# Seven-product matrix scheme in a gated MLP: the output's last block moved from second to last

## The chip, the cores and the metric

The kernel runs on one core of a Trainium2 chip. The metric is the device time of one execution in microseconds (us).

## What is computed

Eight batches of 448 tokens go through a sigmoid attention and then through a gated MLP. Cut to what matters:

```python
scores = q @ k.T / sqrt(64) - log(448)           # 12 heads, head_dim 64
x = sigmoid(scores) @ v                          # 448 x 768 per batch
h = relu(x @ w_in)                               # 448 x 1024
u, v = h[:, :512], h[:, 512:]
v_s = w_spatial @ normalised(v) + b_spatial      # over the tokens
out = (u * v_s) @ w_out                          # 448 x 768
```

Everything is float32. On TensorE a float32 product is made from three products of rounded parts: high x high, low x high and high x low.

## The kernel before

Batches are taken in pairs, m = 0 to 3. A pair goes through attention (scores psc, values pav), through the gate's products (pv, pg), then through the products for u (PSUM tiles ux, uy) and last through the output's products (PSUM tiles o). Pair 0 uses plain products; pairs 1 to 3 use a scheme that makes a 2 x 2 block product from seven block products. Only these three pairs are touched here.

**The scheme.** Both factors are cut into 2 x 2 blocks. For the output, the rows are the 512 channels of the gated values in halves, the columns are the two batches b0 and b1. The weight blocks are called 11, 12, s2, s3, s1, s4 and 22 (s1 to s4 are sums of blocks, made once and kept in DRAM). Each meets one block of the other factor: 11 meets G11, 12 meets G21, s2 meets T2, s3 meets T3, s1 meets T1, s4 meets G22, and 22 meets T4. The gated blocks are G11, G21, G12 and G22, where the first digit is the channel half and the second the batch; T1 = G12 - G11, T3 = G22 - G12, T2 = T3 + G11 = G22 - T1, T4 = G21 - T2. Products 11, s2, s1 and s4 add up in one PSUM sum X, products 12, s3 and 22 add up in another, Y, and after some of them the running sum is copied out, to be added to the other sum later. `by_blocks` (L836) runs through the seven; for the output each has three row blocks i = 0, 1, 2 of six matmuls, so 18 matmuls. X and Y of one i are the two halves of one PSUM tile `o_i`.

**Where the gated blocks come from.** `gated_by_blocks` (L859) does the same with u's weights (two row blocks i, nine matmuls each). Its results, gated by VectorE (`gate`, L898), are ready in the order G11, G22, G12 and last G21. Its local `then` issues the VectorE and ScalarE work after each product: copies and additions of the running sums (r1, r2, r3), the gate, `high` (ScalarE rounds a block to its high part, L901) and `low` (VectorE subtracts the high part, L905). What is not urgent is a generator `rest` (L907) put into a list of jobs, and `spare(n)` takes n steps from it.

**The output.** `output_by_blocks` (L967) has its own `then`: after product 11 it copies the running sum X to r1, after 12 it adds Y to r1 and sends the row to DRAM, and so on; `between` runs after the last row block of s3 and issues the next pair's loads (`more_loads`: a value load, one attention load, another value load) and `next_splits` (six VectorE instructions that split the next pair's first three attention inputs). At L1020 on, each row is sent to DRAM as it is ready.

**What sets the order.** Every engine runs its instructions in the order in which the code issues them (`in_program_order`), and waits on semaphores. SyncE (SP) issues all loads and stores, in order. Seven weight blocks share four places in SBUF: block n + 4 is loaded once block n's product is through (`load_block`). The work tiles come from pools with a few buffers under a tag: raw (4), v (2), tmp (3); a new tile takes the buffer that was given up first and waits for its last reader. The gated blocks sit in the program's tiles `g_2_0` (G11), `g_2_2` (G21), `g_3_0` (G12) and `wval_s` (G22) for pair 1; `ur_1_0`, `ur_1_1`, `ur_1_2` are the running sums.

Of the kernel before, what the change touches and what calls it, by code (L numbers as in the profile page):

```python
# [8 lines left out]
F32 = mybir.dt.float32  # L9
# [26 lines left out]
def attn_gmlp_kernel(  # L36
# [412 lines left out]
    ORDER = ("11", "12", "s2", "s3", "s1", "s4", "22")  # L449
# [24 lines left out]
    def keep_plain(w7, w):  # L474
        for name in NAMES:
            if name in ORDER:
                at = NAMES.index(name) * BLOCK
                nc.sync.dma_start(w7[ORDER.index(name)], w[:, :, at : at + BLOCK].bitcast(F32))

    def output_weight_sums(stage):  # L480
# [13 lines left out]
        def finish(i, name):  # L494
            nc.vector.tensor_sub(low(i).bitcast(F32R), low(i), high(i).bitcast(F32))
            nc.sync.dma_start(w7_out[ORDER.index(name)], stage[:, i])

# [33 lines left out]
    def weight_sums():  # L531
# [14 lines left out]
        keep_plain(w7_u, w_u[0])  # L546
# [288 lines left out]
    PRODUCTS = (("11", X), ("21", W), ("t2", X), ("t3", Y), ("t1", X), ("22", X), ("t4", Y))  # L835

    def by_blocks(flat, stationary, moving, nk, ps, then):

        started = set()
        for pos, (mv, to) in enumerate(PRODUCTS):  # L840
            w = block(flat, pos)
            ops = [(a, k, c) for k in range(nk) for a, c in TERMS]
            for i, out_ps in enumerate(ps[to]):
# [10 lines left out]
                then(pos, i)  # L854
# [5 lines left out]
    def gated_by_blocks(m):  # L860
# [106 lines left out]
    def output_by_blocks(m, final, between):  # L967
# [5 lines left out]
        spare_u = sums.pop("r")[2]  # L973
# [4 lines left out]
        r1 = [spare_u[:, 0], spare_u[:, 1], in_wval(2)]  # L978
        later = {}

        def pieces(name, last):
            t = work.tile([P, 2, 512], F32, tag="tmp", name=f"o{name}_{m}", bufs=3)
            later[name] = [t[:, 0, :S], t[:, 1, :S], in_wval(last)]
# [10 lines left out]
        def then(pos, i):  # L994
            mv = PRODUCTS[pos][0]
            if mv == "11":
                spare(1)
                nc.scalar.copy(r1[i], px[i])  # L998
            elif mv == "21":
                if not i:  # L1000
                    spare(1)
                nc.vector.tensor_add(r1[i], py[i], r1[i])
                leave(b0, i, 0, r1[i])
                spare(1)
                if i == n - 1:
                    spare(99)
                    pieces("r3", 0)
                    pieces("c12", 1)
                    pieces("r2", 2)
            elif mv == "t2":  # L1010
                nc.scalar.copy(later["r2"][i], px[i])
            elif mv == "t3":
                if i == n - 1:
                    between()
            elif mv == "t1":
                r3 = later["r3"][i]
                nc.scalar.copy(r3, px[i])
                nc.vector.tensor_add(r3, py[i], r3)
                leave(b1, i, 1, r3)
            elif mv == "22":  # L1020
                nc.scalar.copy(later["c12"][i], px[i])
                leave(b1, i, 0, later["c12"][i])
            elif mv == "t4":
                r2 = later["r2"][i]
                nc.vector.tensor_add(r2, py[i], r2)
                leave(b0, i, 1, r2)
# [268 lines left out]
    for m in range(B // 2):  # L1295
        if m == 1:
            stage = const.tile([P, 4, 2, BLOCK], F32, tag="w_u", name="stage")
            keep_plain(w7_out, w_out_s)
# [36 lines left out]
        if m:  # L1335
# [86 lines left out]
```

## Time and profile before

| what | value |
|---|---|
| median of three runs | 660.47 us (659.56 to 660.82) |
| the profiled execution | 661.15 us |
| its span | 659.3 us |
| TensorE busy, share of the span | 642.7 us, 97% |
| VectorE busy | 450.5 us, 68% |
| ScalarE busy | 324.9 us, 49% |
| chain that ended last | PE 91%, DVE 6%, ACT 2%, DMA 1% |

The profile names engines PE (TensorE), PEld (its weight loads), DVE (VectorE), ACT (ScalarE), POOL (GpSimd) and SP (SyncE, with its queue SPq). Ends of matmuls are modelled, so a matmul's duration in a row is longer than the step from one to the next. The chain that ended last is followed back from the last instruction to what released it; its share by engine says who set the time. TensorE is nearly always busy, so what is to be looked for is where it is not, and where it is busy at less than full clock.

### The profile page before, as it was taken

What the parts mean: (1) busy time and instruction counts of PE and PEld (TensorE: products, weight loads), DVE (VectorE), ACT (ScalarE), POOL (GpSimd) and SP (SyncE); (2) the same over time, 40 slices, a digit from 0 to 9 for tenths busy, and PEclk for the clock granted to TensorE, in tenths of its full rate; (3) what the DMA queues carried; (4) which work ended last, traced back from release to release, by engine and by line L of the source; (5) the groups of instructions that cost most, each with busy time, mean ns of one, the idle gap of its engine ahead of it and who ended that gap; (6) DMA issues with size and microseconds to landing.
All of it is one profiled execution on the core that took longest, in us unless ns stands there. A gap on an engine that the chain in (4) does not pass through costs nothing.

```text
span 659.3 us, 10184 instructions
## 1 busy us (share of the span) xinstructions
PE 642.7 (97%) x4154; PEld 495.3 (75%) x4154; DVE 450.5 (68%) x629; ACT 324.9 (49%) x410; POOL 28.8 (4%) x63
## 2 busy tenths in 40 slices
PE   8999999999999999997999999999799999999977
PEld 3645889999754588996966658899696666889966
DVE  4989789849478887839476638674836754777562
ACT  5986322323777845224268745512427774542231
POOL 0000010000000002000000002200000000210000
PEclk9999999999999999998999999999799999999989
DMA  8764113565862491044744460012574465002144
GB/s 294 242 200 173 55 41 95 153 247 197 302 241 75 163 366 54 1 144 147 278 171 171 164 277 0 1 49 95 178 275 143 171 229 211 1 1 92 52 141 171
DMA packets 29952, 99.90 MB, mean 152 GB/s; under 512 B 3152, under 2 KB 9808, under 8 KB 29904
## 3 DMA queue, kind: packets, MB, share of 16 engines
q1 hardware_dynamic: 29472, 98.89, 41.6%
q8 instruction: 33, 0.54, 0.3%
q10 hardware_dynamic: 432, 0.34, 0.2%
q14 instruction: 15, 0.12, 0.1%
HBM read 77.20 MB, written 22.02 MB: 150 GB/s over the span
## 4 chain that ended last, share of the span: by engine, by line
PE 91%; DVE 6%; ACT 2%; DMA 1%; issue 0%; SPq 0%; DVEq 0%
PE pv L418 17%; PE pav L1147 15%; PE psc L336 13%; PE o L845 10%; PE pg L779 10%; PE pav L385 5%; PE ux L845 5%; PE pu L418 4%; PE po L418 4%; PE uy L845 3%; PE psc L318 3%; DVE g L898 1%; DVE mlp L905 1%; DMA raw<-qk_dram 1%; ACT x_s L901 1%; PE pg L754 1%
## 5 line engine op out<-in xcount | busy, mean ns | idle before, releaser
L418 PE MATMUL pv<-w_g_s,x_s 128*128 128x512 f32 x504 | 115.4, 391 | 0.0
L418 PEld LDWEIGHTS pv<-w_g_s,x_s 128*128 128x128 f32 x504 | 94.4, 188 | 22.2 <-issue 2.1
L300 ACT ACTIVATE ats<-psc,bias_s 128x896 f32<-128x896 f32 x102 | 95.3, 1007 | 20.2 <-PE pav L1147 13.5
L336 PEld LDWEIGHTS psc<-qks 64*128 64x128 f32 x840 | 77.8, 185 | 15.3 <-issue 5.6
L336 PE MATMUL psc<-qks 64*128 64x448 f32 x840 | 88.9, 366 | 0.0
L1147 PE MATMUL pav<-ats,v 64*64 64x448 f32 x720 | 76.0, 540 | 0.0
L779 PE MATMUL pg<-w_sp_s,mlp 128*128 128x448 f32 x320 | 65.8, 364 | 0.0
L779 PEld LDWEIGHTS pg<-w_sp_s,mlp 128*128 128x128 f32 x320 | 59.8, 188 | 5.3 <-issue 1.2
L1147 PEld LDWEIGHTS pav<-ats,v 64*64 64x64 f32 x720 | 28.2, 133 | 37.4 <-issue 26.4
L845 PE MATMUL o<-x_s,w_out_s 128*128 128x448 f32 x162 | 40.2, 405 | 10.8 <-ACT ur L998 10.8
L286 DVE TENSOR_TENSOR qks<-raw,qks 128x848 fp32r<-128x848 f32 x46 | 47.4, 1041 | 1.1
L845 PEld LDWEIGHTS o<-x_s,w_out_s 128*128 128x128 f32 x162 | 34.0, 213 | 15.7 <-ACT ur L998 13.0
L845 PE MATMUL o<-mlp,w_out_s 128*128 128x448 f32 x216 | 45.3, 366 | 0.0
L123 DVE TENSOR_TENSOR x_s<-pav,x_s 128x896 fp32r<-128x896 f32 x16 | 17.4, 1091 | 40.1 <-ACT x_s L122 40.1
L845 PEld LDWEIGHTS o<-mlp,w_out_s 128*128 128x128 f32 x216 | 41.3, 191 | 2.8
L725 DVE SCALAR_TENSOR_TENSOR mlp<-rv,rstd,mlp 128x512 fp32r<-128x512 f32 (+1 forms) x32 | 23.5, 750 | 17.4 <-ACT mlp L720 16.9
L845 PE MATMUL ux<-x_s,w_u 128*128 128x448 f32 x162 | 33.4, 362 | 0.0
L1147 PE MATMUL pav<-at,v 64*64 64x448 f32 x216 | 32.0, 537 | 0.0
L845 PEld LDWEIGHTS ux<-x_s,w_u 128*128 128x128 f32 x162 | 30.4, 188 | 2.0
L418 PE MATMUL pu<-x_s,w_u_s 128*128 128x448 f32 x144 | 29.1, 362 | 0.0
L418 PEld LDWEIGHTS pu<-x_s,w_u_s 128*128 128x128 f32 x144 | 27.0, 188 | 1.8
L385 PE MATMUL pav<-ats,v 128*64 128x448 f32 (+1 forms) x144 | 27.1, 545 | 0.0
(160 smaller groups left out, 890.2 us busy)
## 6 DMA issues: line engine op xcount, KB each, us to landing
raw<-qk_dram SPq DMA_DIRECT2D x47, 456.0 KB, 5.1
w_u<-w_u SPq DMA_DIRECT2D x21, 768.0 KB, 5.0
w_out_s<-w_out SPq DMA_DIRECT2D x21, 768.0 KB, 11.3
v<-v_dram SPq DMA_DIRECT2D x24, 448.0 KB, 4.1
wraw<-w_in_dram SPq DMA_DIRECT2D x12, 512.0 KB, 4.9
wraw<-w_out_dram SPq DMA_DIRECT2D x6, 512.0 KB, 3.8
w_u<-x_s SPq DMA_DIRECT2D x4, 768.0 KB, 3.6
w_out<-stage SPq DMA_DIRECT2D x4, 768.0 KB, 3.7
```

Of the source, the lines that this page charges most:

```text
L123: nc.vector.tensor_sub(lo, src, hi.bitcast(F32))
L286: nc.vector.tensor_sub(s[:, 1], loaded[b, hp][:, HALF:], s[:, 0].bitcast(F32))
L300: nc.scalar.activation(at, src, AF.Sigmoid, bias=bias_s, scale=QK)
L318: nc.tensor.matmul(psc[odd * HALF : (odd + 1) * HALF, j, :S], raw[rows, :HALF], raw[rows, HALF + Q :], start=True, stop=True,)
L336: nc.tensor.matmul(psc[:, j, :S], st[rows, k : k + P], mv[rows, Q:PART], start=i == 0, stop=i == len(ops) - 1,)
L385: nc.tensor.matmul(pav[heads, odd, :S], vt[rows, t, heads], at[rows, j], start=start, stop=t == NFULL,)
L418: nc.tensor.matmul(ps, st, mv, start=i == 0, stop=i == len(ops) - 1)
L725: nc.vector.scalar_tensor_tensor(lo, rv[rows, i], rstd[rows, i : i + 1], hi.bitcast(F32), op0=ALU.mult, op1=ALU.subtract,)
L754: nc.tensor.matmul(pgs[b, fcs][:, i, :S], vns[NFULL][rows, odd, fc * P : (fc + 1) * P], w_sp_s[rows, NFULL, 1, cols_of(b)], start=(b, fcs) ...
L779: nc.tensor.matmul(pg[:, i, :S], st, mv, start=n == 0 and not ended, stop=n == len(ops) - 1 and ended,)
L845: nc.tensor.matmul(out_ps, stationary(w, i, k)[:, a], moving[mv][k][c], start=(to, i) not in started and n == 0, stop=n == len(ops) - 1, s ...
L1147: ins = nc.tensor.matmul(pavs[pair][heads, i % 2, :S], vt[rows, t if t == NFULL else t + i % 2 * (NFULL + 1), heads], at[rows, j], start=i ...
```

## The change

The order of the seven products is now set per factor. For u it stays as it was (`ORDER_U`); for the output block 12, which needs G21, goes last (`ORDER_OUT`), and the blocks in DRAM are laid out in that order. With it:

- T3 is formed first, then T2 = T3 + G11 and their roundings; the low part of G22, T1 = G22 - T2, T1's parts, T4 and the low part of G21 (now one instruction instead of two halves) move into `rest`.
- In the output's `then`, the copy of a running sum stands ahead of the spare job; three steps of `rest` run after product 11's row blocks, the last one after s2.
- The running sums after s1 (r3) now live in u's third running sum, and the ones after 11 (r1) in u's first; c12 and r2 take new tmp tiles (`rooms`), before all three did.
- `between` is split: after s3 the first value load (for every m, taken out of `more_loads`) and `next_splits`; after s1 the fourth attention load; the second value load after the whole output.
- The rows that end last, and are cut in two for the last store, are now b0's row 0 instead of its row 1.

```diff
-    ORDER = ("11", "12", "s2", "s3", "s1", "s4", "22")
+    ORDER_U = ("11", "12", "s2", "s3", "s1", "s4", "22")
+    ORDER_OUT = ("11", "s2", "s3", "s1", "s4", "22", "12")
...
-        r1, r2 = (work.tile([P, 2, S], F32, tag="v", name=f"ur_{m}_{n}", bufs=2) for n in range(2))
+        r2, r1 = (work.tile([P, 2, S], F32, tag="v", name=f"ur_{m}_{n}", bufs=2) for n in range(2))
...
         def rest():
-            low("t2", g22)
-            yield True
-            nc.vector.tensor_sub(g21, g21, g22)
-            high("t4", g21)
+            high("21", g21, 1)
+            low("22", g22)
+            nc.vector.tensor_sub(g22, g22, g11)
             yield True
             low("t3", g12)
             yield True
-            low("t1", g11)
-            yield True
-            low("t4", g21)
+            high("t1", g22)
+            low("t1", g22)
+            nc.vector.tensor_sub(r2, g21, g11)
+            low("21", g21)
+            yield True
+            high("t4", r2)
+            low("t4", r2)
             yield True
...
                 if i:
                     gate(g22, r3)
                     high("22", g22)
-                    low("22", g22)
             elif mv == "22":
                 gate(g12, px[i], i)
                 if i:
-                    nc.vector.tensor_sub(g11, g12, g11)
-                    high("t1", g11)
                     nc.vector.tensor_sub(g12, g22, g12)
                     high("t3", g12)
+                    nc.vector.tensor_add(g11, g12, g11)
+                    high("t2", g11)
             elif mv == "t4":
                 nc.vector.tensor_add(r2[:, i], py[i], r2[:, i])
                 gate(g21, r2[:, i], i)
-                high("21", g21, i)
                 if not i:
-                    nc.vector.tensor_sub(g22, g22, g11)
-                    high("t2", g22)
-                else:
-                    low("21", g21, 0)
-                    low("21", g21, 1)
+                    high("21", g21, 0)
+                    low("t2", g11)
...
-        def then(pos, i):
-            mv = PRODUCTS[pos][0]
+        def then(mv, i):
             if mv == "11":
+                nc.scalar.copy(r1[i], px[i])
                 spare(1)
-                nc.scalar.copy(r1[i], px[i])
+                if i == n - 1:
+                    rooms()
+            elif mv == "t2":
+                nc.scalar.copy(r2[i], px[i])
+                if i == n - 1:
+                    spare(99)
+            elif mv == "t3":
+                if i == n - 1:
+                    between[0]()
+            elif mv == "t1":
+                nc.scalar.copy(r3[i], px[i])
+                nc.vector.tensor_add(r3[i], py[i], r3[i])
+                leave(b1, i, 1, r3[i])
+                if i == n - 1:
+                    between[1]()
...
-            def between():
-                more_loads(m + 1)
+            def values_and_splits():
+                ahead(value_loads, (m + 1) * 2 * NHP)
                 next_splits()
...
-            output_by_blocks(m, not more, between)
+            def last_raw():
+                ahead(attention_loads, (m + 1) * 2 * NHP + 3)
+
+            output_by_blocks(m, not more, (values_and_splits, last_raw))
+            ahead(value_loads, (m + 1) * 2 * NHP + 2)
```

TensorE's first half of the output products of pair 1, before: `mlp` holds G11, G22, T1 and T2, `x_s` holds G21, T3 and T4.

```order
L845 MATMUL o_0_2611<-mlp_2076,w_out_s 128x448 x6
L845 MATMUL o_1_2612<-mlp_2076,w_out_s 128x448 x6
L845 MATMUL o_2_2613<-mlp_2076,w_out_s 128x448 x6
L845 MATMUL o_0_2611<-x_s,w_out_s 128x448 x6
L845 MATMUL o_1_2612<-x_s,w_out_s 128x448 x6
L845 MATMUL o_2_2613<-x_s,w_out_s 128x448 x6
L845 MATMUL o_0_2611<-mlp_2076,w_out_s 128x448 x6
L845 MATMUL o_1_2612<-mlp_2076,w_out_s 128x448 x6
L845 MATMUL o_2_2613<-mlp_2076,w_out_s 128x448 x6
L845 MATMUL o_0_2611<-x_s,w_out_s 128x448 x6
```

The same after:

```order
L850 MATMUL o_0_2606<-mlp_2076,w_out_s 128x448 x6
L850 MATMUL o_1_2607<-mlp_2076,w_out_s 128x448 x6
L850 MATMUL o_2_2608<-mlp_2076,w_out_s 128x448 x6
L850 MATMUL o_0_2606<-mlp_2076,w_out_s 128x448 x6
L850 MATMUL o_1_2607<-mlp_2076,w_out_s 128x448 x6
L850 MATMUL o_2_2608<-mlp_2076,w_out_s 128x448 x6
L850 MATMUL o_0_2606<-x_s,w_out_s 128x448 x6
L850 MATMUL o_1_2607<-x_s,w_out_s 128x448 x6
L850 MATMUL o_2_2608<-x_s,w_out_s 128x448 x6
L850 MATMUL o_0_2606<-mlp_2076,w_out_s 128x448 x6
```

The product with G21 (x_s, second group of three) is gone from here; s2 (T2, in mlp) follows product 11 at once.

VectorE in pair 1, before, from T1 to T4 (`g_2_0` is G11 and then T1, `g_3_0` G12 and then T3, `wval_s` G22 and then T2, `g_2_2` G21 and then T4):

```order
L942 TENSOR_TENSOR g_2_0_2356<-g_3_0_2412,g_2_0_2356 128x2x448
L944 TENSOR_TENSOR g_3_0_2412<-wval_s_74,g_3_0_2412 128x2x448
L947 TENSOR_TENSOR ur_1_1_2364<-uy_1_0_2442,ur_1_1_2364 128x448
L898 SCALAR_TENSOR_TENSOR g_2_2_2386<-ur_1_1_2364,g_2_2_2386 128x448
L951 TENSOR_TENSOR wval_s_74<-wval_s_74,g_2_0_2356 128x896
L947 TENSOR_TENSOR ur_1_1_2364<-uy_1_1_2443,ur_1_1_2364 128x448
L898 SCALAR_TENSOR_TENSOR g_2_2_2386<-ur_1_1_2364,g_2_2_2386 128x448
L905 TENSOR_TENSOR x_s_70<-g_2_2_2386,x_s_70 128x448 x2
L905 TENSOR_TENSOR mlp_1_2076<-wval_s_74,mlp_1_2076 128x896
L910 TENSOR_TENSOR g_2_2_2386<-g_2_2_2386,wval_s_74 128x2x448
L905 TENSOR_TENSOR x_s_70<-g_3_0_2412,x_s_70 128x2x448
L905 TENSOR_TENSOR mlp_1_2076<-g_2_0_2356,mlp_1_2076 128x896
```

After (`g_3_0` G12 and then T3, `g_2_0` G11 and then T2, `wval_s` G22 and then T1):

```order
L948 TENSOR_TENSOR g_3_0_2412<-wval_s_74,g_3_0_2412 128x2x448
L950 TENSOR_TENSOR g_2_0_2356<-g_3_0_2412,g_2_0_2356 128x2x448
L953 TENSOR_TENSOR ur_1_0_2363<-uy_1_0_2442,ur_1_0_2363 128x448
L903 SCALAR_TENSOR_TENSOR g_2_2_2386<-ur_1_0_2363,g_2_2_2386 128x448
L910 TENSOR_TENSOR mlp_1_2076<-g_2_0_2356,mlp_1_2076 128x896
L953 TENSOR_TENSOR ur_1_0_2363<-uy_1_1_2443,ur_1_0_2363 128x448
L903 SCALAR_TENSOR_TENSOR g_2_2_2386<-ur_1_0_2363,g_2_2_2386 128x448
L910 TENSOR_TENSOR mlp_1_2076<-wval_s_74,mlp_1_2076 128x896
L915 TENSOR_TENSOR wval_s_74<-wval_s_74,g_2_0_2356 128x896
L910 TENSOR_TENSOR x_s_70<-g_3_0_2412,x_s_70 128x2x448
L910 TENSOR_TENSOR mlp_1_2076<-wval_s_74,mlp_1_2076 128x896
L921 TENSOR_TENSOR ur_1_0_2363<-g_2_2_2386,g_2_0_2356 128x896
```

T2's low part moves up from behind G21's to the fifth place, and the low parts of G22 and G21 move down. What follows on VectorE, before:

```order
L1002 TENSOR_TENSOR ur_1_2_2362<-o_1_0_2611,ur_1_2_2362 128x448
L905 TENSOR_TENSOR x_s_70<-g_2_2_2386,x_s_70 128x2x448
L1002 TENSOR_TENSOR ur_1_2_2362<-o_1_1_2612,ur_1_2_2362 128x448
L1002 TENSOR_TENSOR wval_s_74<-o_1_2_2613,wval_s_74 128x448
L279 CAST qks_4_0_2716<-raw_4_0_2605 128x848
L286 TENSOR_TENSOR qks_4_0_2716<-raw_4_0_2605,qks_4_0_2716 128x848
L279 CAST qks_4_1_2719<-raw_4_1_2607 128x848
L286 TENSOR_TENSOR qks_4_1_2719<-raw_4_1_2607,qks_4_1_2719 128x848
L279 CAST qks_4_2_2722<-raw_4_2_2609 128x848
L286 TENSOR_TENSOR qks_4_2_2722<-raw_4_2_2609,qks_4_2_2722 128x848
L1018 TENSOR_TENSOR or3_1_2666<-o_1_0_2611,or3_1_2666 128x448
```

After:

```order
L910 TENSOR_TENSOR x_s_70<-g_2_2_2386,x_s_70 128x2x448
L910 TENSOR_TENSOR x_s_70<-ur_1_0_2363,x_s_70 128x2x448
L279 CAST qks_4_0_2686<-raw_4_0_2600 128x848
L286 TENSOR_TENSOR qks_4_0_2686<-raw_4_0_2600,qks_4_0_2686 128x848
L279 CAST qks_4_1_2689<-raw_4_1_2602 128x848
L286 TENSOR_TENSOR qks_4_1_2689<-raw_4_1_2602,qks_4_1_2689 128x848
L279 CAST qks_4_2_2692<-raw_4_2_2604 128x848
L286 TENSOR_TENSOR qks_4_2_2692<-raw_4_2_2604,qks_4_2_2692 128x848
L1016 TENSOR_TENSOR ur_1_2_2362<-o_1_0_2606,ur_1_2_2362 128x448
L1016 TENSOR_TENSOR ur_1_2_2362<-o_1_1_2607,ur_1_2_2362 128x448
L1016 TENSOR_TENSOR wval_s_74<-o_1_2_2608,wval_s_74 128x448
```

The additions after product 12 (`ur_1_2` and wval, L1002) no longer stand ahead of the six split instructions (`qks`, L279 and L286); the additions after s1 (now into `ur_1_2`, L1016) stand behind them as before.

SyncE in pair 1's output, before (`w_out_s` are weight blocks, `raw` and `v` the next pair's inputs, `out_dram` the stores):

```order
L468 DMA w_out_s<-w_out 128x1536
L992 DMA out_dram<-ur_2_2362 128x448 x2
L992 DMA out_dram<-wval_s 128x448
L468 DMA w_out_s<-w_out 128x1536 x2
L271 DMA v_0_2710<-v_dram 128x896
L266 DMA raw_3_2712<-qk_dram 128x912
L271 DMA v_2_2714<-v_dram 128x896
L992 DMA out_dram<-or_1_2666 128x448 x2
L992 DMA out_dram<-wval_s 128x448
L992 DMA out_dram<-oc_1_2667 128x448 x2
L992 DMA out_dram<-wval_s 128x448
L992 DMA out_dram<-or_1_2668 128x448 x2
```

After:

```order
L271 DMA v_0_2684<-v_dram 128x896
L469 DMA w_out_s<-w_out 128x1536
L999 DMA out_dram<-ur_2_2362 128x448 x2
L999 DMA out_dram<-wval_s 128x448
L266 DMA raw_3_2723<-qk_dram 128x912
L999 DMA out_dram<-oc_1_2639 128x448 x2
L999 DMA out_dram<-othirds_2638 128x448
L999 DMA out_dram<-or_1_2640 128x448 x2
L999 DMA out_dram<-othirds_2638 128x448
L999 DMA out_dram<-ur_1_2364 128x448 x2
L999 DMA out_dram<-wval_s 128x448
L271 DMA v_2_2797<-v_dram 128x896
```

The fourth attention load (`raw`) moves behind the first three stores, which are of the same buffer, and the second value load (`v`) behind all nine.

## Rows read from the trace of the kernel before

**Rows 1.** The page's part 1: busy us, share of the span, instructions.

```profile
PE 642.7 (97%) x4154; PEld 495.3 (75%) x4154; DVE 450.5 (68%) x629; ACT 324.9 (49%) x410; POOL 28.8 (4%) x63
```

**Rows 2.** Waits: who waited for whom, us in total, times, longest us.

```profile
PE o L845 <- ACT ur L998: 10.8, 6, 2.2
```

**Rows 3.** Timeline, TensorE, pair 1: start us, duration us, instruction, [idle before it].

```profile
290.21 7.36 PE L845 MATMUL ux<-x_s,w_u 128*128 128x448 f32 x36
297.41 3.76 PE L845 MATMUL uy<-x,w_u 128*128 128x448 f32 x18
301.01 3.76 PE L845 MATMUL o<-mlp,w_out_s 128*128 128x448 f32 x18
306.21 1.48 PE L845 MATMUL o<-x_s,w_out_s 128*128 128x448 f32 x6 [1.44 <-ACT ur L998]
309.85 4.11 PE L845 MATMUL o<-x_s,w_out_s 128*128 128x448 f32 x12 [2.15 <-ACT ur L998]
...
331.89 1.74 PE L318 MATMUL psc<-raw 64*64 64x448 f32 x16
```

**Rows 4.** Timeline, TensorE, pairs 2 and 3: first and last rows of the output's stretch.

```profile
462.04 3.76 PE L845 MATMUL o<-mlp,w_out_s 128*128 128x448 f32 x18
...
494.20 0.98 PE L318 MATMUL psc<-raw 64*64 64x448 f32 x8
...
624.35 3.76 PE L845 MATMUL o<-mlp,w_out_s 128*128 128x448 f32 x18
...
651.70 3.77 PE L845 MATMUL o<-x_s,w_out_s 128*128 128x448 f32 x18
```

**Rows 5.** Stretches of pair 1: us, busy us (instructions) by engine, granted clock, DMA share, GB/s.

```profile
306.00:308.00 2.00, 1.48 (x6) 1.05 (x6) 2.00 (x3) 0.16 (x1) 0.00 (x0) 1.00 0.76 276
308.00:310.00 2.00, 0.15 (x1) 0.15 (x1) 2.00 (x3) 1.57 (x3) 0.00 (x0) 0.88 0.22 89
310.00:312.00 2.00, 2.00 (x6) 1.79 (x7) 1.93 (x3) 0.23 (x1) 0.00 (x0) 0.50 0.09 33
```

**Rows 6.** Timeline, VectorE and ScalarE, pair 1.

```profile
295.23 1.09 DVE L898 SCALAR_TENSOR_TENSOR wval_s<-ur,wval_s 128x896 f32<-128x896 f32 x1
...
299.52 1.09 DVE L942 TENSOR_TENSOR g<-g,g 128x896 f32<-128x896 f32 x1
300.65 1.09 DVE L944 TENSOR_TENSOR g<-wval_s,g 128x896 f32<-128x896 f32 x1
301.66 0.62 DVE L947 TENSOR_TENSOR ur<-uy,ur 128x448 f32<-128x448 f32 x1
301.77 0.95 ACT L901 CAST x_s<-g 128x896 fp32r<-128x896 f32 x1 [0.18 <-DVE g L944]
302.31 0.62 DVE L898 SCALAR_TENSOR_TENSOR g<-ur,g 128x448 f32<-128x448 f32 x1
302.85 1.09 DVE L951 TENSOR_TENSOR wval_s<-wval_s,g 128x896 f32<-128x896 f32 x1
...
307.31 1.08 DVE L910 TENSOR_TENSOR g<-g,wval_s 128x896 f32<-128x896 f32 x1
308.31 1.08 DVE L905 TENSOR_TENSOR x_s<-g,x_s 128x896 fp32r<-128x896 f32 x1
...
309.27 0.53 ACT L998 COPY ur<-o 128x448 f32<-128x448 f32 x1
...
314.60 0.59 DVE L279 CAST qks<-raw 128x848 fp32r<-128x848 f32 x1
...
318.41 1.04 DVE L286 TENSOR_TENSOR qks<-raw,qks 128x848 fp32r<-128x848 f32 x1
```

**Rows 7.** DMA issues: out<-in, count, KB each, median us from issue to landing.

```profile
raw<-qk_dram SPq DMA_DIRECT2D x47, 456.0 KB, 5.1
w_out_s<-w_out SPq DMA_DIRECT2D x21, 768.0 KB, 11.3
v<-v_dram SPq DMA_DIRECT2D x24, 448.0 KB, 4.1
out_dram<-ur SPq DMA_DIRECT2D x6, 224.0 KB, 1.9
```

**Rows 8.** Timeline, TensorE: the next pair's first value products.

```profile
340.96 1.74 PE L1147 MATMUL pav<-ats,v 64*64 64x448 f32 x16
```

More of the change, by code (lines that the diff above doesn't have):

```diff
@@ L472, in plain, with keep_plain @@
         return w[:, a, at : at + BLOCK].bitcast(F32)
-    def keep_plain(w7, w):
+    def keep_plain(w7, order, w):
         for name in NAMES:
-            if name in ORDER:
+            if name in order:
                 at = NAMES.index(name) * BLOCK
-                nc.sync.dma_start(w7[ORDER.index(name)], w[:, :, at : at + BLOCK].bitcast(F32))
+                nc.sync.dma_start(w7[order.index(name)], w[:, :, at : at + BLOCK].bitcast(F32))
     def output_weight_sums(stage):
@@ L495, in finish @@
             nc.vector.tensor_sub(low(i).bitcast(F32R), low(i), high(i).bitcast(F32))
-            nc.sync.dma_start(w7_out[ORDER.index(name)], stage[:, i])
+            nc.sync.dma_start(w7_out[ORDER_OUT.index(name)], stage[:, i])
         add(0, part("21", 0), part("21", 1))
@@ L539, in keep @@
         def keep(name, i):
-            nc.sync.dma_start(w7_u[ORDER.index(name)], staged(i).bitcast(F32))
+            nc.sync.dma_start(w7_u[ORDER_U.index(name)], staged(i).bitcast(F32))
         def low(i, t):
@@ L544, in low @@
             nc.vector.tensor_sub(st[:, 1], t, st[:, 0].bitcast(F32))
-        keep_plain(w7_u, w_u[0])
+        keep_plain(w7_u, ORDER_U, w_u[0])
         nc.vector.tensor_add(t0, plain(w_u[0], "21", 0), plain(w_u[0], "21", 1))
@@ L834, in attn_gmlp_kernel @@
     X, W, Y = "x", "w", "y"
-    PRODUCTS = (("11", X), ("21", W), ("t2", X), ("t3", Y), ("t1", X), ("22", X), ("t4", Y))
+    OPERANDS = {
+        "11": ("11", X), "12": ("21", W), "s2": ("t2", X), "s3": ("t3", Y),
+        "s1": ("t1", X), "s4": ("22", X), "22": ("t4", Y),
+    }
     def by_blocks(flat, stationary, moving, nk, ps, then):
         started = set()
-        for pos, (mv, to) in enumerate(PRODUCTS):
+        for pos, name in enumerate(ORDER_U if flat is flat_u else ORDER_OUT):
+            mv, to = OPERANDS[name]
             w = block(flat, pos)
@@ L853, in by_blocks @@
                 started.add((to, i))
-                then(pos, i)
+                then(mv, i)
             if pos + HELD < NB:
@@ L972, in output_by_blocks, with rooms @@
         px, py = ([ps[:, a, :S] for ps in tiles] for a in range(2))
-        spare_u = sums.pop("r")[2]
+        u1, _, u3 = sums.pop("r")
         def in_wval(i):
             return wval_s[:, i * S : (i + 1) * S].bitcast(F32)
[L978 to L983, printed above, removed]
+        r1 = [u1[:, 0], u1[:, 1], in_wval(2)]
+        r3 = [u3[:, 0], u3[:, 1], in_wval(0)]
+        r2, c12 = [], []
+        def rooms():
+            thirds, c, r = (
+                work.tile([P, 2, 512], F32, tag="tmp", name=f"o{name}_{m}", bufs=3)[:, :, :S]
+                for name in ("thirds", "c12", "r2")
+            )
+            r2.extend([r[:, 0], r[:, 1], thirds[:, 0]])
+            c12.extend([c[:, 0], c[:, 1], thirds[:, 1]])
         def leave(b, i, row, src):
             e = 2 * i + row
-            if final and row and b == b0:
+            if final and not row and b == b0:
                 h = S // 2
@@ L992, in leave, with then @@
                 nc.sync.dma_start(out[b, e], src)
-        def then(pos, i):
-            mv = PRODUCTS[pos][0]
+        def then(mv, i):
             if mv == "11":
+                nc.scalar.copy(r1[i], px[i])
                 spare(1)
-                nc.scalar.copy(r1[i], px[i])
+                if i == n - 1:
[13 more added lines that the diff above has]
+                    between[1]()
+            elif mv == "22":
+                nc.scalar.copy(c12[i], px[i])
+                leave(b1, i, 0, c12[i])
+            elif mv == "t4":
+                nc.vector.tensor_add(r2[i], py[i], r2[i])
+                leave(b0, i, 1, r2[i])
             elif mv == "21":
-                if not i:
-                    spare(1)
                 nc.vector.tensor_add(r1[i], py[i], r1[i])
                 leave(b0, i, 0, r1[i])
[L1004 to L1026, printed above, removed]
         by_blocks(
@@ L1072, in more_loads @@
         n = m * 2 * NHP
-        if m > 1:
-            ahead(value_loads, n)
         ahead(attention_loads, n + 3)
@@ L1297, in attn_gmlp_kernel @@
             stage = const.tile([P, 4, 2, BLOCK], F32, tag="w_u", name="stage")
-            keep_plain(w7_out, w_out_s)
+            keep_plain(w7_out, ORDER_OUT, w_out_s)
             jobs.append(output_weight_sums(stage))
```

## The prediction

> **What bounds the kernel now.** The page first: TensorE is busy 97% of the span [rows 1], so only two things can be won, its idle time and its time at the lower clock. The list of waits comes next: TensorE's only large wait for another engine is on the output's products, 10.8 us in six waits, put down to ScalarE's copy of a running sum [rows 2]. The timeline then shows the place. In pair 1 the output's stretch runs from 301.01 to 331.89, 30.88 us [rows 3]. It has 126 matmuls, and 18 of them step on by 3.60 us (297.41 to 301.01, no wait between), so it needs 25.20; 5.68 us are lost. Two waits stand in it, both in product 12: its first row block starts at 306.21 where 304.61 was possible (1.60), its second at 309.85 where 307.41 was possible (2.44). The other 1.6 us is the clock: granted 1.00 until 308, 0.50 from 310, 2 us for 6 matmuls [rows 5]; it fell after the second wait, and after the first one six matmuls still ran at full rate. Pair 2 takes 462.04 to 494.20, 32.16 us, and loses 6.96; pair 3 needs 27.35 to the start of its last 18 where 21.60 would do, and loses 5.75 [rows 4]. The three stretches lose 18.4 us, 12.1 by waits and 6.3 by the clock.
>
> The reason is VectorE, which has no gap from 299.52 on [rows 6]: G21 is the last block that u gives, and product 12 stands second. Product 12's first block needs G21's high part, and ScalarE's copies of r1 are queued between late casts: the second copy runs at 309.27 only, behind a cast of T4 that waits for VectorE [rows 6].
>
> **What the change takes away.** After it, product 11 is followed by s2, which needs T2, so I walk along VectorE with the steps of the rows: 1.00 us from one 896-wide instruction to an independent one (307.31 to 308.31), 1.13 to one that needs its result (299.52 to 300.65), for 448-wide ones 0.65 (301.66 to 302.31) and 0.54 (302.31 to 302.85), a cast on ScalarE 0.95, a copy 0.53 [rows 6]. The last gate of G12 can start when the 36 matmuls of T1 and G22's blocks have ended, 290.21 + 7.36 = 297.57 [rows 3]; before, G22's low part stood in front. Then: T3 at 298.27, T2 at 299.40, addition and gate of G21's first half 300.41 and 301.06, T2's low part 301.60 to 302.69. T2's high part is there at 299.40 + 1.09 + 0.95, so 301.46. s2 may begin at 304.61: 1.9 us to spare. The copies of r1 no longer stand behind a cast that is late; the second and third need G21's second cast ahead of them, ready at 303.9, and end near 304.9 and 305.4, against 305.81 and 307.01 when s2's row blocks want them. So both waits of product 12 go.
>
> What is next? G21's second addition and gate 302.60 and 303.25, G22's low part 303.79, T1 304.91, T3's low part 305.91 to 306.99, T1's low part 306.98, T4 307.98, G21's low part 308.98. s3 begins at 308.21 and needs T3's low part and the first copy of r2. That copy goes into G12's buffer, waits for 306.99 and ends near 307.55: 0.65 us to spare, the thinnest margin here. T4's low part needs ScalarE, which first copies the third row of r2 into G11's old buffer, free when T4 has been formed (309.07); copy and cast end at 310.5, the low part runs 310.50 to 311.58. s1, s4's operand, 22 and 12 have theirs long before. Weight blocks come later than they are asked for by more than 6 us: s4's block is issued near 304.8 as before, when the DMA share falls to 0.22 by 308 to 310 [rows 5], and is wanted at 315.4. The number of VectorE instructions falls by one (two halves of G21's low part become one); the rest of the change of names and buffers costs nothing as long as these margins hold.
>
> **What it adds.** The six splits of the next pair now follow T4's low part at once: 311.50, and 3.81 + 0.96 later (314.60 to 318.41, and the step from a split's subtraction to the next instruction) VectorE is free for the additions of r3, 316.27 to 316.89. TensorE reaches s4 at 301.01 + 4 x 3.60 = 315.41. In the built program s4's first matmul waits for that addition: it reads Y's half of the tile o_0 while s4 writes X's half, and the dependence is by tile. Before, the same wait is there but long met. The trace shows such a wait by tile: product 12 writes Y and waited for the copy of X [rows 2, 3]. So s4 waits 1.5 us, in pairs 1 and 2; pair 3 has no next pair and no splits. Behind it on TensorE stands all the rest of the output. From both sides: nothing, if VectorE is 1.5 us faster than my walk or the rows wait by half tiles, and some 2 us if each of the 21 VectorE steps takes 0.02 more; I take 1.5, the walk itself.
>
> The rule on this is in the Trainium skill, PSUM — Partial Sum Buffer, PSUM bank collisions raise a hardware error: engines have to be kept apart by bank and quadrant, and different banks may be used together. X's and Y's halves are 512 floats apart, a bank each, so by that rule s4 needn't wait; the trace goes by tile, and the wait stays in the sum.
>
> SyncE: the fourth attention load now waits for two stores of r3 to land. These are issued near 317 and 317.6, land 1.9 us later [rows 7], so the load goes at 319.5 and lands 5.1 later, at 324.6. It is wanted by the next pair's second group of short scores, 0.75 us after the output's end, at 301.01 + 26.7 + 0.75 = 328.5: 3.9 us to spare. Queued behind it are only stores. The second value load waits for r1's second store, landed 1.6 us after the output's end, and is there 4.1 us on, at 5.7 [rows 7]; the first value products come 9.07 us after the end (331.89 to 340.96) [rows 3, 8]. The three loads queued behind it start about 1 us later than before. None is on the path.
>
> **The sum.** Pair 1: 5.68 - 1.5 = 4.2. Pair 2: 6.96 - 1.5 = 5.5. Pair 3: 5.75. Together 15.4 us. The end is unchanged: three additions, half stores. The profiled execution took 661.15, so 645.75; the median of the runs is 0.68 below it, so 645.1.
>
> **The rivals.**
> - *A, no wait at s4.* The walk is off by 1.5 us, or the wait is not there: 642.1. Against it the built program's wait. 0.06.
> - *B, the wait at s4 halves the clock.* Priced by pair 1's and pair 2's time at 0.50 in the trace, 5.68 - 4.04 = 1.64 and 6.96 - 4.04 = 2.92: 645.1 + 4.6 = 649.7. For it: the clock did fall within this stretch [rows 5]. Against it: it fell after 4.04 us lost of 5.24, not after the first 1.60. 0.13. By the Trainium skill, TensorE: Matmul & The Clock Gate, A second HAM failure mode: psum-queue depth-cycling, frequent short idling between groups of matmuls is enough to bring the lower clock; here the first of two waits was not.
> - *C, the change does not do it all:* s2 or s3 still waits. The thinnest margin is 0.65 us; a walk 1.65 us longer makes s3 wait 1 us in each of three pairs, 648.1, and up to 650 with s4 later by as much. 0.09.
> - *D, slower.* The fourth attention load is late: each us beyond its 3.9 of cover stalls TensorE in pairs 1 and 2. With the longest landing in the table, 11.3 us [rows 7], it is 2.3 each, 649.7. It has to land 17 us after its issue before the change is slower than 661.8. 0.05, of which 0.02 on that side.
>
> The forecast itself has 0.67. The range 641.5 to 650.0 holds A, B, most of C and the first half of D, 0.85 or so in all. A measurement can tell 0.2%, 1.3 us; faster by more 0.96, within 0.02, slower 0.02.
>
> **What would show it.** In the profile after: no wait on ScalarE's copy of r1 and s2 right after 11 without a gap; granted clock 1.00 throughout the output; stretches of 26.7, 26.7 and, to the start of the last 18, 21.6 us; one wait of 1.5 us in pairs 1 and 2 at s4, for an addition on VectorE just behind six splits. A gap ahead of s3, a clock of 0.50 behind s4, or a short score waiting for `raw` would make it wrong.

## The result and the profile after

The changed kernel takes 645.48 us (median of four runs, 645.17 to 646.03), against 660.18 us (659.56 to 660.82) for the kernel before in the same comparison: a ratio of 0.9778, 95% interval 0.9761 to 0.9795. The forecast was 645.1.

The page of the profile after: its span, part 1 (busy us, share of the span, instructions), of part 2 the granted clock in 40 slices, of part 4 the chain by engine.

```profile
span 644.1 us, 10173 instructions
...
PE 636.0 (99%) x4154; PEld 490.3 (76%) x4154; DVE 450.4 (70%) x626; ACT 324.5 (50%) x410; POOL 28.8 (4%) x63
...
PEclk9999999999999999999999999999999999999999
...
PE 93%; DVE 6%; ACT 0%; issue 0%; ACTq 0%
```

TensorE's busy time fell by 6.7 us with the same 4154 matmuls [rows 1]. That is near the 6.3 that the forecast took for what the half clock added to them; the granted clock is 0.9 or more in all 40 slices, and 1.00 over the whole execution. ScalarE's share of the chain is 0%, where it was 2%. Of TensorE's waits for another engine one on the output's products is left, in place of the 10.8 us of [rows 2]:

```profile
PE o L850 <- DVE ur L1016: 3.0, 2, 1.5
```

The timeline of TensorE in pair 1 (start, duration, instruction, [idle before it]) answers to [rows 3]:

```profile
300.38 7.36 PE L850 MATMUL o<-mlp,w_out_s 128*128 128x448 f32 x36
307.58 3.76 PE L850 MATMUL o<-x_s,w_out_s 128*128 128x448 f32 x18
311.18 3.76 PE L850 MATMUL o<-mlp,w_out_s 128*128 128x448 f32 x18
316.44 3.88 PE L850 MATMUL o<-mlp,w_out_s 128*128 128x448 f32 x18 [1.50 <-DVE ur L1016]
320.16 7.37 PE L850 MATMUL o<-x_s,w_out_s 128*128 128x448 f32 x36
327.46 1.73 PE L318 MATMUL psc<-raw 64*64 64x448 f32 x16
```

Products 11 and s2 are now one row of 36 matmuls, without a gap; s3 and s1 follow; then the wait of 1.50 ahead of s4. Behind it the granted clock stays at 1.00 (columns as in [rows 5]):

```profile
318.00:320.00 2.00, 2.00 (x12) 1.88 (x11) 0.00 (x0) 1.02 (x2) 0.00 (x0) 1.00 0.61 211
```

Pair 2, first and last rows with the wait, and then pair 3:

```profile
457.62 7.36 PE L850 MATMUL o<-mlp,w_out_s 128*128 128x448 f32 x36
...
473.69 3.88 PE L850 MATMUL o<-mlp,w_out_s 128*128 128x448 f32 x18 [1.50 <-DVE ur L1016]
...
484.69 1.74 PE L318 MATMUL psc<-raw 64*64 64x448 f32 x16
...
614.86 7.36 PE L850 MATMUL o<-mlp,w_out_s 128*128 128x448 f32 x36
...
632.86 7.36 PE L850 MATMUL o<-x_s,w_out_s 128*128 128x448 f32 x36
```

Pair 1's stretch takes 27.08 us where it took 30.88. Pair 2 (457.62 to 484.69) takes 27.07 where it took 32.16, with the same wait at s4. Pair 3 has none: from 614.86 to the start of its last 18 (half of the 36 that start at 632.86, so 3.60 later) it takes 21.60 where it took 27.35 [rows 3, 4]. That is 3.80 + 5.09 + 5.75 = 14.64 us. Between the stretches nothing moved: from the end of one to the start of the next it is 130.16 and 130.17 us, before 130.15 and 130.15. The other 0.6 of the 15.2 us by which the span is shorter stands ahead of pair 1's output, which starts at 300.38 instead of 301.01; in the executions below that start lies between 300.19 and 301.03, so it is the spread of single executions and not the change.

VectorE and ScalarE in the same place answer to [rows 6]:

```profile
297.64 1.09 DVE L948 TENSOR_TENSOR g<-wval_s,g 128x896 f32<-128x896 f32 x1
298.77 1.09 DVE L950 TENSOR_TENSOR g<-g,g 128x896 f32<-128x896 f32 x1
...
300.98 1.08 DVE L910 TENSOR_TENSOR mlp<-g,mlp 128x896 fp32r<-128x896 f32 x1
...
305.30 1.09 DVE L910 TENSOR_TENSOR x_s<-g,x_s 128x896 fp32r<-128x896 f32 x1
...
310.00 1.09 DVE L910 TENSOR_TENSOR x_s<-ur,x_s 128x896 fp32r<-128x896 f32 x1 [0.52 <-ACT x_s L906]
311.01 0.59 DVE L279 CAST qks<-raw 128x848 fp32r<-128x848 f32 x1
...
314.81 1.04 DVE L286 TENSOR_TENSOR qks<-raw,qks 128x848 fp32r<-128x848 f32 x1
315.77 1.15 DVE L1016 TENSOR_TENSOR ur<-o,ur 128x448 f32<-128x448 f32 x2
```

```profile
301.78 0.53 ACT L1003 COPY ur<-o 128x448 f32<-128x448 f32 x1
303.76 0.53 ACT L1003 COPY ur<-o 128x448 f32<-128x448 f32 x1
...
306.49 0.97 ACT L1008 COPY or<-o 128x448 f32<-128x448 f32 x2
```

The second copy of r1 (L1003), which ran at 309.27 before, 8.26 us after the stretch's start, runs at 303.76, 3.38 us after it. T4's low part (310.00) ends a chain of VectorE steps without a gap but the 0.52; six splits follow, then the additions of r3 (L1016), of which the first releases s4.

### The profile page after: what moved, and what is told of

It is laid out like the page before. It is cut to its first block, busy times and chain, and to the rows that moved or that the text cites. A ratio compares the mean times of both kernels' runs of the same rounds, so it can differ in the third digit from the quotient of the medians.

```text
span 644.1 us, 10173 instructions
## 1 busy us (share of the span) xinstructions
PE 636.0 (99%) x4154; PEld 490.3 (76%) x4154; DVE 450.4 (70%) x626; ACT 324.5 (50%) x410; POOL 28.8 (4%) x63
## 4 chain that ended last, share of the span: by engine, by line
PE 93%; DVE 6%; ACT 0%; issue 0%; ACTq 0%
PE pv L418 18%; PE pav L1147 15%; PE psc L336 14%; PE pg L780 10%; PE o L850 7%; PE ux L850 7%; PE pav L385 5%; PE pu L418 4%; PE po L418 4%; PE uy L850 4%; PE psc L318 3%; DVE qks L286 1%; DVE mlp L910 1%; DVE x_s L910 1%; PE pg L755 1%; DVE g L903 1%
## 5 line engine op out<-in xcount | busy, mean ns | idle before, releaser
L286 DVE TENSOR_TENSOR qks<-raw,qks 128x848 fp32r<-128x848 f32 x46 | 47.4, 1041 | 1.0
L850 PE MATMUL o<-x_s,w_out_s 128*128 128x448 f32 x162 | 33.4, 362 | 0.0
L850 PEld LDWEIGHTS o<-x_s,w_out_s 128*128 128x128 f32 x162 | 30.4, 188 | 2.0
L300 ACT ACTIVATE at<-psc,bias_s 128x896 f32<-128x896 f32 x18 | 17.9, 1009 | 18.6 <-PE psc L318 18.4
```

The source lines that it names most:

```text
L286: nc.vector.tensor_sub(s[:, 1], loaded[b, hp][:, HALF:], s[:, 0].bitcast(F32))
L300: nc.scalar.activation(at, src, AF.Sigmoid, bias=bias_s, scale=QK)
L850: nc.tensor.matmul(out_ps, stationary(w, i, k)[:, a], moving[mv][k][c], start=(to, i) not in started and n == 0, stop=n == len(ops) - 1, s ...
```

## Experiments

Every kernel below computes the whole output; where work is repeated, the expectation says so. Pair 1's start shifts by some tenths between executions, so lengths are compared, not positions. The new buffers and the new places of the loads stay in all of them (10 moves one load); what they would do without the rest was not tried.

**1. The wait at s4 taken away.** The six splits are issued after s1, behind the additions of r3.

```diff
             def values_and_splits():
                 ahead(value_loads, (m + 1) * 2 * NHP)
-                next_splits()
             def last_raw():
                 ahead(attention_loads, (m + 1) * 2 * NHP + 3)
+                next_splits()
```

> The changed kernel, but the six split instructions are issued after the three row blocks of s1 instead of after s3. Theory (what is left of the loss is s4 waiting for r3's addition on VectorE behind the splits): the addition runs as soon as s1's copy is there, s4 follows s1 without a gap in pairs 1 and 2, 2 x 1.66 us less than the changed kernel's 645.5, so 642.2. Rival (the wait only moves on, to product 12 behind the splits, or to the next pair's first scores): 645 to 646, with a gap there.

Measured: 642.08 us (641.82 to 642.42), ratio to the kernel before 0.9718 (0.9698 to 0.9737), clock 1.00. TensorE, then VectorE, in pair 1:

```profile
311.15 7.36 PE L850 MATMUL o<-mlp,w_out_s 128*128 128x448 f32 x36
318.35 7.36 PE L850 MATMUL o<-x_s,w_out_s 128*128 128x448 f32 x36
325.64 1.73 PE L318 MATMUL psc<-raw 64*64 64x448 f32 x16
```

```profile
313.12 0.62 DVE L1016 TENSOR_TENSOR ur<-o,ur 128x448 f32<-128x448 f32 x1 [2.05 <-ACT ur L1015]
...
316.12 0.59 DVE L279 CAST qks<-raw 128x848 fp32r<-128x848 f32 x1
```

The addition runs at 313.12, as soon as its operand is copied, and s1 and s4 are one row of 36. The stretch is 25.29 us, 1.79 less than after the change; two pairs make 3.6, the difference of the spans (644.1 and 640.5). So the wait is the place of the addition behind the splits, and this version is faster than both kernels.

**2. The order alone.** The new order, with the sums formed as before (`rest` and the gated `then` of the old code) and the copies behind the spare job.

```diff
         def rest():
-            high("21", g21, 1)
-            low("22", g22)
-            nc.vector.tensor_sub(g22, g22, g11)
+            low("t2", g22)
+            yield True
+            nc.vector.tensor_sub(g21, g21, g22)
+            high("t4", g21)
             yield True
...
             if mv == "11":
-                nc.scalar.copy(r1[i], px[i])
                 spare(1)
+                nc.scalar.copy(r1[i], px[i])
                 if i == n - 1:
+                    spare(99)
                     rooms()
```

> Of the change, only the order of the output's products (with the buffers and loads that it needs): T1, T3, T2 and T4 are formed as before, and r1's copies stand behind the spare jobs as before. Theory (the order alone gains next to nothing, since T2's low part comes behind G21's on VectorE and the second copy of r1 behind T4's cast): s2's first row block waits some 2.4 us for T2's low part, its second some 1.6 us for the copy, the clock halves after them, no wait at s4: 5.7 to 7 us lost per pair, 658 to 662. Rival (putting G21's product last is what gains): 645 to 648.

Measured: 660.70 us (ten runs), ratio 1.0003 (0.9994 to 1.0013), clock 0.986. TensorE, pair 1, from product 11 to s3:

```profile
300.48 3.76 PE L850 MATMUL o<-mlp,w_out_s 128*128 128x448 f32 x18
305.69 0.68 PE L850 MATMUL o<-mlp,w_out_s 128*128 128x448 f32 x2 [1.45 <-ACT ur L1006]
306.92 1.86 PE L850 MATMUL o<-mlp,w_out_s 128*128 128x448 f32 x4 [0.55 <-DVE mlp L910]
309.32 4.61 PE L850 MATMUL o<-mlp,w_out_s 128*128 128x448 f32 x12 [0.55 <-ACT ur L1006]
313.77 3.77 PE L850 MATMUL o<-x_s,w_out_s 128*128 128x448 f32 x18
```

The waits have moved from 12 to s2, for the copies of r1 and for T2's low part: 313.77 - 300.48 is 13.29 us where 7.20 would do, so 6.1 are lost, against 5.68 before. The order by itself only changes which product stands second.

**3. Order and copies, old sums.** As 2, with the copies ahead.

```diff
             if mv == "11":
                 nc.scalar.copy(r1[i], px[i])
                 spare(1)
                 if i == n - 1:
+                    spare(99)
                     rooms()
```

> The changed kernel, but T1, T3, T2 and T4 are formed as before the change. Theory (the sums are needed for the gain): s2's first row block waits some 2.4 us in each pair for T2's low part, its third some 0.4 for a copy; s4's wait is gone since TensorE is later; 642.2 + 3 x 2.8 = 650.6 at full clock, up to 655 if the clock halves. Rival (order and copies are enough): 645.5.

Measured: 653.40 us (652.79 to 654.06), ratio 0.989 (0.9872 to 0.9907), clock 0.995. In every pair s2 waits 1.45 for a copy of r1, which still stands behind late casts, and then 0.55 for T2's low part. TensorE's last 16 matmuls of s2, in pairs 1 and 2:

```profile
306.71 3.89 PE L850 MATMUL o<-mlp,w_out_s 128*128 128x448 f32 x16 [0.56 <-DVE mlp L910]
...
465.12 5.07 PE L850 MATMUL o<-mlp,w_out_s 128*128 128x448 f32 x16 [0.55 <-DVE mlp L910]
```

The time is as expected, by waits of another make: the 2.4 us of the first row block I had put down to T2's low part alone. The 16 matmuls take 3.72 in pair 1 (310.43 - 306.71), where 3.20 would do, at a granted clock of 1.00; the third row block's copy of r1 ends only at 309.06, and 0.4 for it was expected. In pairs 2 and 3 they take 4.90, with the granted clock down to 0.50: the same waits lowered it there, for 1.2 us each, and not in pair 1.

**4. Order and sums, copies behind the spare job.**

```diff
             if mv == "11":
-                nc.scalar.copy(r1[i], px[i])
                 spare(1)
+                nc.scalar.copy(r1[i], px[i])
```

> The changed kernel, but each copy of r1 stands behind the spare job again. Theory (with the new sums no cast in front of the copies is late by more than a few tenths): s2's first row block waits 0.4 us in each pair, pairs 1 and 2 get it back at s4: 645.9. Rival (the copies carry a good part of the gain): 649 and more, with waits for r1's copies of over 1 us and a lower clock.

Measured: 646.38 us (646.23 to 646.72), ratio 0.9784 (0.9768 to 0.98), clock 1.00. TensorE, pair 1, s2 and s4:

```profile
304.23 3.98 PE L850 MATMUL o<-mlp,w_out_s 128*128 128x448 f32 x18 [0.20 <-ACT ur L1004]
...
316.34 3.87 PE L850 MATMUL o<-mlp,w_out_s 128*128 128x448 f32 x18 [0.93 <-DVE ur L1016]
```

s2 waits 0.20, TensorE comes to s4 0.57 later than in the changed kernel, and s4 waits 0.57 less: the stretches of pairs 1 and 2 stay at 27.07 and 27.06, and only pair 3's is longer, by 0.57. With the new sums the copies' place is worth that; the medians differ by 0.9, which is no more than noise between two comparisons (the ratios' intervals overlap). With the old sums (2 against 3) it was worth 7.3.

**5. Sums and copies, old order.**

```diff
-    ORDER_OUT = ("11", "s2", "s3", "s1", "s4", "22", "12")
+    ORDER_OUT = ("11", "12", "s2", "s3", "s1", "s4", "22")
```

> The changed kernel with the old order of the output's products (12 second again); sums and copies stay new. Theory (the new sums put G21's low part behind those of T2, G22, T3 and T1): product 12's first row block waits from 304.4 to 309.5, some 5.1 us in each pair, and the clock halves after it for 1.6 to 3 us; no wait at s4: 642.2 + 3 x 6.7 to 8 = 662 to 666, slower than the kernel before. Rival (sums and copies gain whatever the order): 645 to 650.

Measured: 666.00 us (665.46 to 666.84), ratio 1.0083 (1.0066 to 1.01), clock 0.985. Product 12 in pair 1:

```profile
309.35 5.97 PE L850 MATMUL o<-x_s,w_out_s 128*128 128x448 f32 x16 [4.99 <-DVE x_s L910]
```

With G21's low part moved to the end of `rest`, 12 in second place waits 5.0 us for it in each pair, and behind it the granted clock is 0.50 (the 16 matmuls take 5.80 in pair 1 where 3.20 would do). s4 still waits 0.7 in pairs 1 and 2, which I had not expected: T4's cast stands on ScalarE behind the copies of r2, and these come as late as s2 does (the last at 319.00), so T4's low part runs at 320.40 only, and the splits behind it.

**6, 7, 8. A longer wait at s4.** How near is the 1.5 us to the lower clock? One or more of the splits' instructions are done twice in pairs 1 and 2, so that the addition comes later. Once the whole first split is repeated, then its cast alone (`n < 1`), then the casts of the first two (`n < 2`).

```diff
                     attention_splits(*units[(m + 1) * 2 * NHP + n])
+                    if m and not n:
+                        raw = loaded[units[(m + 1) * 2 * NHP]][:, HALF:]
+                        s = parts_of[units[(m + 1) * 2 * NHP]]
+                        nc.vector.tensor_copy(s[:, 0], raw)
+                        nc.vector.tensor_sub(s[:, 1], raw, s[:, 0].bitcast(F32))
```

```diff
+                    if m and n < 1:
+                        u = units[(m + 1) * 2 * NHP + n]
+                        nc.vector.tensor_copy(parts_of[u][:, 0], loaded[u][:, HALF:])
```

> The changed kernel; in pairs 1 and 2 the first of the three splits is done twice, which leaves the result as it is. Theory (s4 waits for r3's addition behind the splits, and a single wait of some 3 us doesn't lower the clock): each wait grows by 1.6, to 3.1 us, 645.5 + 3.2 = 648.7, granted clock 1.00 after it. Rival B of the prediction (the wait at s4 halves the clock once it is long enough): 652 to 655, clock 0.50 after the wait. If s4 does not wait for the splits: 645.5.

> The changed kernel with the first split's cast done twice in pairs 1 and 2, 0.6 us more of VectorE ahead of the addition that s4 waits for; nothing is left out. Theory (the clock falls only after a wait well above 1.5 us): s4 waits 2.1 us in pairs 1 and 2, granted clock stays at 1.00, 645.5 + 2 x 0.6 = 646.7. Rival (the 1.5 us of the changed kernel is just below the point from which the clock falls): 1.2 to 2.9 us more in each of the two pairs, 649 to 652.5, with a granted clock near 0.5 behind s4's first block.

> The changed kernel with the first two splits' casts done twice in pairs 1 and 2, 1.2 us more of VectorE ahead of the addition that s4 waits for; nothing is left out. Theory: s4 waits 2.7 us in pairs 1 and 2; granted clock still 1.00: 645.5 + 2 x 1.2 = 647.9. Rival (between 1.5 and 2.7 us lies the point from which the clock falls, as it did with 3.2 us): 650.3 to 653.7, with a granted clock near 0.5 behind s4's first block.

Measured: the whole split 652.93 us (651.95 to 653.72), one cast 651.6 us (651.53 to 651.99, and one run of 647.66), two casts 649.99 us (649.73 to 651.91). s4 in pairs 1 and 2, first of the kernel with one cast, then of that with two, then of that with the whole split:

```profile
317.74 5.46 PE L850 MATMUL o<-mlp,w_out_s 128*128 128x448 f32 x18 [2.15 <-DVE ur L1016]
...
477.19 5.47 PE L850 MATMUL o<-mlp,w_out_s 128*128 128x448 f32 x18 [2.13 <-DVE ur L1016]
```

```profile
317.69 5.46 PE L850 MATMUL o<-mlp,w_out_s 128*128 128x448 f32 x18 [2.78 <-DVE ur L1016]
...
477.79 3.87 PE L850 MATMUL o<-mlp,w_out_s 128*128 128x448 f32 x18 [2.78 <-DVE ur L1016]
```

```profile
318.33 6.65 PE L850 MATMUL o<-mlp,w_out_s 128*128 128x448 f32 x18 [3.21 <-DVE ur L1016]
...
480.05 5.46 PE L850 MATMUL o<-mlp,w_out_s 128*128 128x448 f32 x18 [3.22 <-DVE ur L1016]
```

And stretches with the columns of [rows 5]: first one of pair 1 with one cast, then one of pair 1 and one of pair 2 with two casts:

```profile
318.00:320.00 2.00, 2.00 (x6) 1.78 (x6) 0.74 (x2) 0.00 (x0) 0.00 (x0) 0.50 0.74 275
```

```profile
320.00:322.00 2.00, 2.00 (x6) 1.78 (x6) 0.00 (x0) 0.47 (x1) 0.00 (x0) 0.50 0.54 153
...
480.00:482.00 2.00, 2.00 (x12) 1.87 (x11) 0.00 (x0) 0.83 (x2) 0.00 (x0) 1.00 0.64 124
```

Starts taken from one another, s4's 18 matmuls step on by:

| kernel | wait in pairs 1, 2 | 18 matmuls, pair 1 | pair 2 |
|---|---|---|---|
| copies behind (4) | 0.9 | 3.71 | 3.71 |
| changed kernel | 1.50 | 3.72 | 3.71 |
| one cast | 2.15, 2.13 | 5.30 | 5.31 |
| two casts | 2.78 | 5.30 | 3.71 |
| whole split | 3.21, 3.22 | 6.49 | 5.30 |

So my theory, that a single wait of up to 3.2 us leaves the clock alone, fell in all three. The rival held with the whole split and with one cast, and in one pair of two with two casts, whose 649.99 lies just under its 650.3. The clock stayed at 1.00 behind the waits of 1.50 and fell behind those of 2.15 and 2.13, for 1.6 us a time, and for up to 2.8 behind the longer ones. It does not fall by the length alone: two casts wait longer than one and lost it in one pair of two, and one of the four runs with one cast took 647.66 at a clock of 0.999 (the others 0.994), near the 646.7 of a clock that stays up. What else decides it isn't settled. Of the 6.1 us by which the span with one cast is longer, 1.3 are wait and 3.2 clock; 0.65 is a later start of pair 1's output, and 1.0 stands behind the last store's issue, which these runs don't explain.

**9. Is the wait by whole tiles?** X of row block i + 1 shares a tile with Y of i; the instructions stay the same.

```diff
-        tiles = [banks(f"o_{m}_{i}") for i in range(n)]
-        px, py = ([ps[:, a, :S] for ps in tiles] for a in range(2))
+        tiles = [banks(f"o_{m}_{i}") for i in range(n + 1)]
+        px = [tiles[i][:, 0, :S] for i in range(n)]
+        py = [tiles[i + 1][:, 1, :S] for i in range(n)]
```

> The changed kernel, but X of row block i + 1 shares a PSUM tile with Y of row block i instead of its own Y (four tiles). The instructions are the same. Theory (waits go by whole tiles): s1's second and third row blocks now wait for r3's addition of the row block ahead, in pairs 1 and 2 for the one behind the splits, s4 about 3.8 us later, in pair 3 about 3 us: 656 at full clock, up to 661. Rival (waits go by bank): as the changed kernel, 645.5, or better by s4's wait.

Measured: 664.32 us, one run, clock 0.987. TensorE in pair 1, s1 (6, 6 and the first 6 of 24) and s4:

```profile
311.77 1.37 PE L850 MATMUL o<-mlp,w_out_s 128*128 128x448 f32 x6
316.52 2.32 PE L850 MATMUL o<-mlp,w_out_s 128*128 128x448 f32 x6 [3.38 <-DVE ur L1017]
320.12 6.74 PE L850 MATMUL o<-mlp,w_out_s 128*128 128x448 f32 x24 [1.28 <-DVE ur L1017]
```

s1's second row block waits 3.38 for the addition that reads the first block's Y, its third 1.28 for the next. It needs neither; it only writes the other half of the same tile. So the wait goes by tile and went along with the tile. The time lies above the 656 to 661 of the theory, so I had the mechanism and too small a price: the stretches of pairs 1 and 2 grow by 6.45 us each where 3.8 was expected, pair 3's by 5.2 where it was 3. The wait behind the splits is longer, since s1 is reached earlier than s4, the clock falls behind it (6 matmuls in 2.32), and the next row block, then pair 3's two, wait 1.28 each for an addition alone; s3, too, takes 0.5 longer in each pair, for a copy of r2.

**10. The fourth attention load without cover.** It is issued after the whole output.

```diff
             def last_raw():
-                ahead(attention_loads, (m + 1) * 2 * NHP + 3)
+                pass
             output_by_blocks(m, not more, (values_and_splits, last_raw))
+            ahead(attention_loads, (m + 1) * 2 * NHP + 3)
```

> The changed kernel, but the next pair's fourth attention load is issued after the whole output instead of after s1. Theory (the load is hidden only by its early issue): issued near 328.5, it lands 3 to 5 us later, and the second short score, wanted at 328.2, waits 3.5 to 5 us in pairs 1 and 2: 652 to 656, up to 661 if the clock halves. Rival (something else hides it): 645.5.

Measured: 656.93 us, one run, clock 0.995. TensorE, the next pair's scores:

```profile
327.66 1.72 PE L318 MATMUL psc<-raw 64*64 64x448 f32 x12
332.29 1.75 PE L318 MATMUL psc<-raw 64*64 64x448 f32 x4 [2.90 <-DMA raw<-qk_dram]
```

The load goes out at 328.81, and TensorE stands until 332.29; the granted clock is 0.55 to 0.59 from 332 to 336. The changed kernel issues it at 319.03, 9.6 us earlier in its stretch, and has no such wait.

## Why the forecast was right, point by point

**The walk along VectorE** held. Moved by the 0.63 of the stretch's earlier start: T3 298.27 (forecast 298.27), T2 299.40 (299.40), T2's low part 301.61 (301.60), T3's low part 305.93 (305.91), T4's low part 310.63 (310.50), the first split 311.64 (311.50), the addition of r3 316.40 (316.27). The only slip is 0.13 us at T4's low part: T4 came 0.05 later than forecast, and ScalarE's copy ahead of the cast started 0.10 after T4's end instead of with it. Two of the forecast's sums are some hundredths off: 297.57 + 0.65 gives 298.22 for T3, not 298.27 (the gate ahead of it started 0.04 later, which covers it), and T2's high part comes to 301.44, not 301.46. Adding steps of neighbouring rows, with one value for dependent and one for independent instructions, carried over 21 instructions.

**The waits of product 12** went, with the half clock behind them. s2 has T2's low part at 302.06 and starts at 303.98, 1.9 us later, as forecast. s3 has its copy of r2 near 307.0 and starts at 307.58, 0.56 us later (forecast 0.65): the thin margin held, rival C with its 648.1 to 650 did not come. Experiments 2 to 5 show that the parts do not add up. Each median is set against that of the kernel before in its own comparison: order alone 0.1 us slower, with copies 7.2 faster, with sums 14.2, with both 14.7, and sums and copies without the order 5.8 slower. Weight blocks held nothing up: the one for s4 went out at 304.18, and the two issued there landed after 4.2 us (median), some 6.4 ahead of s4; the forecast's "come later than they are asked for" means this cover.

**The new wait at s4** is 1.50 where 1.5 was forecast, in pairs 1 and 2 and not in 3, for the addition named. Experiment 1 removes it and gives rival A's time, 642.08 against 642.1; A itself failed because the wait is there. Experiment 9 shows why: the wait goes by tile. By the Trainium skill, PSUM — Partial Sum Buffer, PSUM bank collisions raise a hardware error, different banks may be used together. The wait in the trace is the program's dependence on a tile, two banks wide (1.50 us here, 3.38 in experiment 9), and the measurement stands.

**The sum** was 15.4, the stretches give 14.64. The term mis-sized is the stretch with the wait: 27.08 and 27.07 where 26.7 was forecast. 0.09 of it is the step from the last matmul to the next pair's first score, there without any wait (25.29 in experiment 1, not 25.20); 0.16 is the start behind the wait (316.44 is 1.66 after the possible 314.78), and 0.12 the first matmuls after it. The last two are costs of a wait that a row's idle figure does not hold; [rows 3] had the first of them, 1.60 us lost at a wait of 1.44. So pairs 1 and 2 gained 3.80 and 5.09 where 4.2 and 5.5 were forecast, and pair 3 the 5.75 forecast. The medians fell by 14.70, as the stretches say. That the forecast of 645.1 is off by only 0.4 is in part luck: in this comparison the kernel before took 660.18, 0.3 less than the 660.47 that the forecast started from. The profiled execution hit its 645.75 (645.78) by luck as well, since it started pair 1's stretch 0.6 earlier than the one before.

**Rival B** did not come true at 1.50 us, but was nearer than its argument said. That argument took from [rows 3, 5] that the clock fell only after two waits, 4.04 us together; experiments 6 to 8 lower it with a single wait of 2.1, and the second of the two in [rows 3] is itself 2.15 long. Its price was right: 1.64 and 2.92 per pair, measured 1.6 and 2.8 a time. The rule weighed with it (the Trainium skill, TensorE: Matmul & The Clock Gate, A second HAM failure mode: psum-queue depth-cycling) speaks of frequent short idling between groups of matmuls. One wait of 1.50 us in a stretch left the clock at 1.00 here, and one of 2.1 lowered it without being frequent.

**Rival D**: the fourth attention load goes out at 319.03 (forecast 318.9 in this frame), lands 4.7 us later near 323.7 and is wanted at 328.2; no wait, with a cover of 4.5 us. Experiment 10 shows that the rival's mechanism is real once the cover is gone. The second value load goes out 1.54 us after the output's end (forecast 1.6), without a wait.

SyncE in pair 1, the two loads:

```profile
319.03 0.34 SPq L266 DMA_DIRECT2D raw<-qk_dram  x1
...
329.00 0.34 SPq L271 DMA_DIRECT2D v<-v_dram  x1
```

## What to carry to other kernels

When a product that waits is moved to the end, walk the engines that feed it once more with the steps of neighbouring rows: here the order by itself was worth nothing; with what now stands second formed earlier it brought 14.2 of the 14.7 us, with only the copies moved ahead 7.2. Look for what is queued ahead of each releasing instruction, and for tiles of which two halves are in use at once; here moving six splits behind three additions (experiment 1) gives another 3.4 us. Price a wait on TensorE with the clock behind it, not by its length alone.

## What the hardware showed that I had not expected

A single wait of 2.1 us on TensorE, between long rows of matmuls at full rate, was enough to lower the granted clock to 0.50 for about 3 us (18 matmuls in 5.30 us instead of 3.71), and 1.50 us at the same place was not (3.72). Near that point the outcome differs between pairs and executions of one kernel: with 2.78 us the clock fell in one pair of two, and waits of 1.45 and 0.55 close together (experiment 3) lowered it in pairs 2 and 3 but not in pair 1.
